# Loading the first 256 columns of w1 in two halves and regrouping the first four units of a dense-SiLU-dense kernel

## The chip, the cores and the metric

The kernel runs on one core of one Trainium2 chip. The core has a matrix engine (TensorE, PE in the profile), a vector engine (DVE), a scalar engine (ACT), GpSimd (POOL) and SyncE (SP), which here only issues transfers. Sixteen DMA engines move data between HBM and the core's SBUF. Transfers are issued from two places, SP and ACT, and each has its own DMA queue (q1 and q10 in the profile); both queues feed the same sixteen engines.

The metric is the device time of one execution in microseconds. Before the change it is 126.83 us, the median of three runs (126.76 to 126.91).

## The reference

A two-layer feed-forward block in bf16, x of 2048 x 640, w1 of 640 x 1728, w2 of 1728 x 640:

```
h = jnp.einsum("bsd,df->bsf", x, w1)
h = _silu(h)
out = jnp.einsum("bsf,fd->bsd", h, w2)
```

## The kernel before

The program writes its order by hand. A small `Plan` (lines 21 to 72) collects operations in program order. Each engine then runs its own operations in that order, and waits on a semaphore only where an operation names another as its dependency. Each transfer, or group of transfers, has a semaphore of its own. Nothing is reordered by a scheduler, so the order in the source is the order of each engine.

The first product is computed transposed: h's columns lie on partitions, x's rows along the free axis. For this x is needed transposed (`xT_sb`, five tiles of 128 of the 640 inner columns by 2048 rows). Rows are worked in four chunks of 512 (`SCH`), w1's 1728 columns in 13 column tiles of 128 and a last one of 64.

A *unit* (line 205) is one column tile against some rows. It takes the next of eight PSUM banks in turn (`take_bank`), and issues five matmuls that accumulate over the 640 inner columns (line 209). Then ACT computes a sigmoid of the bank (line 193), and DVE multiplies the bank by it into `hT_sb` (line 196). The first matmul of a unit carries all the unit's waits: for its rows of xT, for its column tile of w1 (`w1_deps`, line 183) and for its bank.

The head of the program fills the core's memory:

- x's first 512 rows come as four tiles of 128 rows (`load_x0`, line 144), issued in turn from SP, ACT, SP, ACT. TensorE transposes them (line 167), and DVE and ACT copy the results to `xT_sb` (lines 173 and 175). Five and a bit warm-up matmuls on a constant precede them (line 158).
- w1 comes in groups of column tiles (`w1_cuts`, line 136, and `load_w1`, line 148). The first group, column tiles 0 and 1, is issued from ACT, behind its two tiles of x. The other groups, tiles 2 and 3, 4 to 7 and 8 to 13, are issued from SP, which first waits until the third tile of x has landed.
- The other rows of x are transposed on the way by the DMA engines (line 231), issued from SP after a wait for the group of column tiles 4 to 7; w2 is loaded between them (lines 238 and 241).

The first four units work on half chunks: column tiles 0 and 1 against the first 256 rows, then column tiles 0 and 1 against the next 256 (`XE` is 256). They stand in lines 244 to 246. From column tile 2 on, each unit takes a whole chunk of 512 rows (line 248). Then come the chunks 1 to 3, the last column tile for all chunks (line 219), and the second product (line 289) with its evictions and stores.

Of the kernel before, what the change touches and what calls it, by code (L numbers as in the profile page):

```python
# [20 lines left out]
class Plan:  # L21
# [9 lines left out]
    def add(self, eng, emit, deps=(), group=None):  # L31
        op = Op(eng, emit, [d for d in deps if d is not None], group)
        self.ops.append(op)
        return op
# [40 lines left out]
def bass_standalone__dense_activation_silu__prompt_kernel(  # L75
# [19 lines left out]
    FT = FR + 1  # L95
# [7 lines left out]
    with ExitStack() as es:  # L103
# [29 lines left out]


        XE = 2 * P
        w1_cuts = [0, 2, 4, 8, FT]
        id_a = add("pool", lambda e: e.memset(ident[:, :], 0.0))
        id_b = add("pool", lambda e: e.affine_select(
            out=ident[:, :], in_=ident[:, :], compare_op=ALU.not_equal, fill=1.0,
# [4 lines left out]
        def load_x0(eng, j):  # L144
            return add(eng, lambda e: e.dma_start(  # L145
                out=x0_sb[:, j, :], in_=x0_v[:, j, :]), group=f"x0_{j}")

        def load_w1(eng, g, deps=()):
            f0, f1 = w1_cuts[g] * P, min(w1_cuts[g + 1] * P, F)
            return add(eng, lambda e: e.dma_start(  # L150
                out=w1_sb[:, :, f0:f1], in_=w1_v[:, :, f0:f1]), deps, group=f"w1_{g}")

        x0_of = [load_x0(eng, j) for j, eng in enumerate(("sp", "act", "sp", "act"))]
        w1_dma = [load_w1("act", 0)] + [load_w1("sp", g, [x0_of[2]]) for g in (1, 2, 3)]

        ones = nc.const_aps.tensor(1.0, [P, SCH], bf16)
        for n in [SCH] * 5 + [2 * P]:
# [47 lines left out]
        def unit(sc, ft, c0, n):  # L205
            b = take_bank()
            cols = slice(sc * SCH + c0, sc * SCH + c0 + n)
            for dt in range(DT):
                pe = add("pe", lambda e, dt=dt: e.matmul(  # L209
                    ps[:, b, 0:n], lhsT=w1_sb[:, dt, ft * P:(ft + 1) * P], rhs=xT_sb[:, dt, cols],  # L210
                    start=(dt == 0), stop=(dt == DT - 1)),
                    x_deps(sc, c0, n) + w1_deps(ft) + bank_free[b] if dt == 0 else ())
            silu(b, [(slice(0, P), ft, cols)], n, pe)
# [15 lines left out]
        for sc in range(1, NSC):  # L229
            for dt in range(DT):  # L230
                x_dma[sc] = add("sp", lambda e, sc=sc, dt=dt: e.dma_start_transpose(
                    out=xT_sb[:, dt, sc * SCH:(sc + 1) * SCH],
                    in_=xf[sc * SCH:(sc + 1) * SCH, dt * P:(dt + 1) * P]),
                    [w1_dma[2]], group=f"x{sc}")
            if sc == 2:
                half = FR // 2
                for a, z in ((0, half), (half, FR)):
                    w2_dma.append(add("sp", lambda e, a=a, z=z: e.dma_start(
                        out=w2_sb[:, a:z, :], in_=w2_v[:, a:z, :]), group="w2"))
                for hh in range(2):  # L240
                    w2_dma.append(add("sp", lambda e, hh=hh: e.dma_start(
                        out=w2_sb[hh * H:(hh + 1) * H, FR, :], in_=w2[FR * P:F, :]), group="w2"))

        for c0 in (0, XE):
            for ft in range(2):
                unit(0, ft, c0, XE)
        for ft in range(2, FR):
            unit(0, ft, 0, SCH)
# [116 lines left out]
```

## Time and profile before

| What | Value |
|---|---|
| median of three runs | 126.83 us (126.76 to 126.91) |
| time of the profiled execution | 127.35 us |
| its span, first to last instruction | 126.0 us |
| TensorE busy | 121.2 us, 96% of the span |
| DVE, ACT busy | 47.6 and 41.5 us |
| granted TensorE clock | 1.000 |
| DMA moved | 10.41 MB in 18665 packets |
| ACT's DMA queue (q10) | 1232 packets, 0.79 MB |
| issue of the first w1 group on ACT, to landing | 4.3 us |
| issue of w1's tiles 2 and 3 on SP, to landing | 4.9 us |

The profiled execution's time is 1.35 us longer than its span, and 0.52 us above the median of the runs. Positions are given in microseconds from the start of the span. Matmuls are pipelined, so the busy time of one matmul is longer than its distance from the next: in the steady part 512-column matmuls follow each other at about 0.216 us (49 matmuls and the pipeline's end in 10.74 us, with a few records missing). A wait in the profile is the idle time of an engine before an instruction, with what released it. A wait is only worth something where the chain of work that ended last runs through it.

### The profile page before, as it was taken

The page shows a single profiled execution, that of the slowest core. Times are in us where ns is not written, and L with a number is a line of the kernel's source. Part 1 is how long each engine was busy: PE and PEld are TensorE (multiplying, and loading weights), DVE is VectorE, ACT ScalarE, POOL GpSimd, SP SyncE. Part 2 cuts the span into 40 slices and gives each one's busy share as a digit, 9 for nine tenths or more (in the row PEclk, how much of TensorE's full clock was granted, in tenths as well). Part 3 has the DMA queues.
Part 4 walks back from the last instruction along what each step waited for, and adds up shares of the span by engine and source line. Part 5 has one row for each costly group of instructions (what it writes and reads, how often), then busy time and mean ns, then how long its engine had stood idle before and what let it go on. Part 6 is the DMA issues. An engine that isn't in the chain of part 4 may idle for free.

```text
span 126.0 us, 2112 instructions
## 1 busy us (share of the span) xinstructions
PE 121.2 (96%) x905; PEld 57.9 (46%) x910; DVE 47.6 (38%) x74; ACT 41.5 (33%) x73; POOL 0.7 (1%) x6
## 2 busy tenths in 40 slices
PE   7689999999999999999999999999999999999992
PEld 2564444444444444444444444444444444445482
DVE  0454666666666666666674020202020210202022
ACT  4444555555555555555550010101010110101021
POOL 2000000000000000000000000000000000000000
PEclk9999999999999999999999999999999999999999
DMA  4898825379970000000000001113230200112415
GB/s 127 237 271 303 99 53 113 87 182 382 280 136 0 5 0 3 0 0 0 0 0 5 0 0 23 35 21 117 102 109 0 104 0 21 26 21 72 156 65 148
DMA packets 18665, 10.41 MB, mean 83 GB/s; under 512 B 11744, under 2 KB 18656, under 8 KB 18656
## 3 DMA queue, kind: packets, MB, share of 16 engines
q1 hardware_dynamic: 17424, 9.49, 28.5%
q10 hardware_dynamic: 1232, 0.79, 2.1%
q8 instruction: 7, 0.11, 0.4%
q14 instruction: 2, 0.02, 0.0%
HBM read 5.16 MB, written 2.62 MB: 62 GB/s over the span
## 4 chain that ended last, share of the span: by engine, by line
PE 91%; DMA 6%; issue 0%; SPq 0%; DVE 0%
PE ps L289 46%; PE ps L209 43%; DMA w_sb<-in_w_dram 4%; DMA x_sb<-in_x_dram 2%; PE ps L219 2%; SPq L145 0%; DVE o_sb L300 0%
## 5 line engine op out<-in xcount | busy, mean ns | idle before, releaser
L209 PE MATMUL ps<-xT_sb,w_sb 128*128 128x512 bf16 (+1 forms) x265 | 56.2, 371 | 1.6 <-DMA w_sb<-in_w_dram 1.3
L196 DVE TENSOR_TENSOR hT_sb<-ps,sig_sb 128x512 bf16<-128x512 f32 (+2 forms) x58 | 39.0, 673 | 23.2 <-ACT sig_sb L193 22.8
L289 PE MATMUL ps<-w_sb,hT_sb 64*128 64x512 bf16 (+2 forms) x486 | 47.3, 352 | 0.0
L193 ACT ACTIVATE sig_sb<-ps 128x512 bf16<-128x512 f32 (+1 forms) x56 | 32.6, 582 | 27.7 <-PE ps L209 26.6
L209 PEld LDWEIGHTS ps<-xT_sb,w_sb 128*128 128x128 bf16 x270 | 26.3, 98 | 31.2 <-DVE xT_sb L173 1.2
L289 PEld LDWEIGHTS ps<-w_sb,hT_sb 64*128 64x128 bf16 x486 | 23.1, 94 | 23.9
L300 DVE CAST o_sb<-ps 128x512 bf16<-128x512 f32 (+2 forms) x9 | 5.7, 632 | 37.6 <-PE ps L289 37.6
L302 ACT CAST o_sb<-ps 128x512 bf16<-128x512 f32 (+2 forms) x9 | 4.8, 539 | 38.6 <-PE ps L289 38.6
L289 PE MATMUL ps<-hT_sb,w_sb 64*128 64x512 bf16 x108 | 12.3, 376 | 0.0
L289 PEld LDWEIGHTS ps<-hT_sb,w_sb 64*128 64x128 bf16 x108 | 5.1, 94 | 6.6 <-issue 0.4
L300 DVE CAST oT_sb<-ps 128x512 bf16<-128x512 f32 x2 | 1.4, 692 | 11.7 <-PE ps L289 11.7
L302 ACT CAST oT_sb<-ps 128x512 bf16<-128x512 f32 x2 | 1.2, 586 | 13.6 <-PE ps L289 13.6
L158 PE MATMUL ps<-const-bfloat16-1.0 128*128 128x512 bf16 (+1 forms) x6 | 2.5, 588 | 0.8 <-PEq L350 0.8
L173 DVE COPY xT_sb<-ps 128x384 bf16<-128x384 bf16 x4 | 1.4, 358 | 3.2 <-PE ps L167 3.2
L219 PE MATMUL ps<-xT_sb,w_sb 128*64 128x512 bf16 x20 | 2.3, 381 | 0.0
L167 PE MATMUL ps<-ident,x_sb 128*128 128x128 bf16 x20 | 2.0, 267 | 0.1
L175 ACT COPY xT_sb<-ps 128x256 bf16<-128x256 bf16 x4 | 1.4, 372 | 2.0 <-PE ps L167 2.0
L167 PEld LDWEIGHTS ps<-ident,x_sb 128*128 128x128 bf16 x20 | 1.6, 125 | 0.8 <-DMA x_sb<-in_x_dram 0.8
L219 PEld LDWEIGHTS ps<-xT_sb,w_sb 128*64 128x64 bf16 x20 | 1.0, 110 | 1.2 <-issue 0.4
L158 PEld LDWEIGHTS ps<-const-bfloat16-1.0 128*128 128x128 bf16 x6 | 0.7, 133 | 1.9 <-issue 1.9
L142 ACT ACT_TABLE_LOAD x1 | 1.3, 1283 | 0.7 <-PEq L350 0.7
L141 DVE MEMSET warm_sb<- 128x32 f32 x1 | 0.1, 85 | 0.8 <-PEq L350 0.8
(7 smaller groups left out, 1.1 us busy)
## 6 DMA issues: line engine op xcount, KB each, us to landing
out_dram<-o_sb SPq DMA_DIRECT2D x14, 160.0 KB, 1.9
w_sb<-in_w_dram SPq DMA_DIRECT2D x1, 1120.0 KB, 7.7
w_sb<-in_w_dram SPq DMA_DIRECT2D x1, 960.0 KB, 5.7
w_sb<-in_w_dram SPq DMA_DIRECT2D x1, 880.0 KB, 8.0
w_sb<-in_w_dram SPq DMA_DIRECT2D x1, 640.0 KB, 6.3
x_sb<-in_x_dram SPq DMA_DIRECT2D x2, 160.0 KB, 2.5
x_sb<-in_x_dram ACTq DMA_DIRECT2D x2, 160.0 KB, 2.9
w_sb<-in_w_dram ACTq DMA_DIRECT2D x1, 320.0 KB, 4.3
```

Source lines behind the costliest of these rows:

```text
L142: add("act", lambda e: e.activation(out=warm_sb[:, :], in_=warm_sb[:, :], func=ACT.Sigmoid), [warm])
L158: add("pe", lambda e, n=n: e.matmul(ps[:, NBANK - 1, 0:n], lhsT=ones[:, 0:P], rhs=ones[:, 0:n], start=True, stop=True))
L167: t = add("pe", lambda e, j=j, b=b, dt=dt, d0=d0: e.transpose(ps[:, b, :].bitcast(bf16)[:, (dt - d0) * P:(dt - d0 + 1) * P], x0_sb[:, j, d ...
L173: c = add("dve", lambda e, src=src, dst=dst: e.tensor_copy(out=dst, in_=src), [t])
L175: c = add("act", lambda e, src=src, dst=dst: e.copy(out=dst, in_=src), [t])
L193: a = add("act", lambda e: e.activation(out=sig_sb[:, s, 0:n], in_=ps[:, b, 0:n], func=ACT.Sigmoid), [pe, sig_free[s]])
L196: v = add("dve", lambda e, rows=rows, ft=ft, cols=cols: e.tensor_tensor(out=hT_sb[rows, ft, cols], in0=ps[rows, b, 0:n], in1=sig_sb[rows, ...
L209: pe = add("pe", lambda e, dt=dt: e.matmul(ps[:, b, 0:n], lhsT=w1_sb[:, dt, ft * P:(ft + 1) * P], rhs=xT_sb[:, dt, cols], start=(dt == 0), ...
L219: pe = add("pe", lambda e, dt=dt, hh=hh: e.matmul(ps[hh * H:(hh + 1) * H, b, :], lhsT=w1_sb[:, dt, FR * P:F], rhs=xT_sb[:, dt, (sc + hh) * ...
L289: pe = add("pe", lambda e, b=b, n=n, lhsT=lhsT, rhs=rhs, ft=ft: e.matmul(ps[:, b, 0:n], lhsT=lhsT, rhs=rhs, start=(swap == 0 and ft == 0), ...
L300: ev = add("dve", lambda e, b=b, n=n, dst=dst: e.tensor_copy(out=dst, in_=ps[:, b, 0:n]), [pe])
L302: ev = add("act", lambda e, b=b, n=n, dst=dst: e.copy(out=dst, in_=ps[:, b, 0:n]), [pe])
```

## The change

The first group of w1's columns is cut in two: column tile 0 and column tile 1 are two transfers, one behind the other on ACT's queue. The groups on SP keep their columns and only shift in number. The first four units are regrouped: column tile 0 against rows 0 to 255 and 256 to 511, then column tile 1 against both. Through `w1_deps` each column tile waits for its own transfer. The wait of x's transposes is written from the end of the list, and means the same group of column tiles (4 to 7) as before.

```diff
-        w1_cuts = [0, 2, 4, 8, FT]
+        w1_cuts = [0, 1, 2, 4, 8, FT]
...
-        w1_dma = [load_w1("act", 0)] + [load_w1("sp", g, [x0_of[2]]) for g in (1, 2, 3)]
+        w1_dma = [load_w1("act", 0), load_w1("act", 1)] + [load_w1("sp", g, [x0_of[2]]) for g in (2, 3, 4)]
...
-                    [w1_dma[2]], group=f"x{sc}")
+                    [w1_dma[-2]], group=f"x{sc}")
...
-        for c0 in (0, XE):
-            for ft in range(2):
+        for ft in range(2):
+            for c0 in (0, XE):
                 unit(0, ft, c0, XE)
```

## The prediction

> **What bounds the kernel now.** I read the page first, then the chain of waits, then the opening 14 us in slices with the DMA queues beside them. The page's table of engine shares says that TensorE is busy nearly always:
>
> ```profile
> PE 121.2 (96%) x905; PEld 57.9 (46%) x910; DVE 47.6 (38%) x74; ACT 41.5 (33%) x73; POOL 0.7 (1%) x6
> ```
>
> So the only time to win or lose is where TensorE stands still, and the chain that ended last (start, length, what) says where:
>
> ```profile
> 1.19 2.73 DMA x_sb<-in_x_dram
> 3.92 0.02 issue
> 3.94 4.93 DMA w_sb<-in_w_dram
> 8.87 0.05 issue
> 8.92 0.82 PE ps L209 x3
> ...
> 63.05 2.28 PE ps L219 x20
> 65.33 58.47 PE ps L289 x594
> ```
>
> The reader is to see that two transfers make the head of the chain. x0's third tile lands at 3.92; this lets SP issue column tiles 2 and 3 of w1 at 3.94; they land at 8.87. From 8.92 to 123.80 there is nothing but TensorE. Whatever delays the landing at 8.87 delays the end by as much, and whatever happens in front of it is free unless it lasts beyond it. Call that landing the gate.
>
> The order of time in front of the gate, TensorE alone (start, length, work, idle before it and what ended it):
>
> ```profile
> 4.78 0.45 PE L167 MATMUL ps<-ident,x_sb 128*128 128x128 bf16 x5
> 6.25 2.35 PE L209 MATMUL ps<-xT_sb,w_sb 128*128 128x256 bf16 x20 [1.02 <-DMA w_sb<-in_w_dram]
> 8.92 1.25 PE L209 MATMUL ps<-xT_sb,w_sb 128*128 128x512 bf16 x4 [0.32 <-DMA w_sb<-in_w_dram]
> ```
>
> The 20 matmuls at 6.25 are the four units that the change regroups. They waited 1.02 us for the first w1 transfer, ended at 8.60, and then TensorE waited 0.32 us more for the gate. Both waits are on w1, but only the second is on the chain: the first is not.
>
> The DMA engines in the same stretch (window, then the busy sums; the last two columns are the share of 16 engines and GB/s):
>
> ```profile
> 4.00:5.00 1.00, 0.85 (x13) 0.68 (x11) 0.72 (x3) 0.84 (x3) 0.00 (x0) 1.00 0.79 218
> 5.00:6.00 1.00, 0.23 (x5) 0.05 (x1) 0.36 (x1) 0.41 (x2) 0.00 (x0) 1.00 0.72 178
> 6.00:7.00 1.00, 0.75 (x7) 0.71 (x8) 0.00 (x0) 0.00 (x1) 0.00 (x0) 1.00 0.99 268
> ```
>
> They are nearly full, so more DMA work here has little room. Who used them, from the queue table (packets, MB, share of 16 engines) of the window 4 to 5, where ACT's queue is alone:
>
> ```profile
> q10 hardware_dynamic: 427, 0.22, 78.6%
> ```
>
> And, for a price, of the window 18 to 22, where SP's queue carries transposes of x alone:
>
> ```profile
> q1 hardware_dynamic: 1684, 0.40, 46.3%
> ```
>
> **The change part by part.**
>
> *The split of the transfer.* One transfer of [128, 5, 256] columns has 128 x 5 = 640 rows of 512 B; two of 128 columns have 1280 rows of 256 B. The bytes stay, the packets double. The price of a 512 B packet: 78.6% of 16 engine-us over 427 packets = 29.5 ns. A plain 256 B load is not in this trace. Lower bound: the transposes, whose packets average 0.40 MB / 1684 = 238 B, took 46.3% of 64 engine-us over 1684 = 17.6 ns, in another kind of transfer. Upper bound: no cheaper than 512 B, 29.5 ns. I take the middle, 23.6 ns, since one row has the right size and the other the right kind. Extra DMA work: (1280 x 23.6 - 640 x 29.5) ns / 16 = 0.71 us; with the ends 0.23 and 1.18 us.
>
> What can hide it: the engines' idle share while SP's transfer comes up. In quarter slices from 5.00 to 6.25 the share was 0.71, 0.73, 0.73, 0.70 and 0.96, so 1.17 x 0.25 = 0.29 us stood empty. I let all of it be filled, because from 6 to 7 the engines reach 0.99. The rest competes with the gate's own 640 packets, which begin at about 5.1: 0.71 - 0.29 = **0.42 us later at the gate**. Ends: 0.23 - 0.29, taken as 0, and 1.18 with nothing filled.
>
> [...]
>
> *One more DMA issue on ACT.* The issue of the w1 transfer took 0.46 us, from 1.84 to 2.30. A second one ends at about 2.76. Behind it on ACT stands the first copy of xT, which began at 3.86 because the transposes were late. Cover 1.1 us, cost nothing; without the cover 0.46 us, at a place that is in front of the gate anyway.
>
> *SP and POOL.* SP issues the same transfers in the same order; the transposes of x still wait for the transfer of column tiles 4 to 7. POOL is untouched. The transfer for tiles 4 to 7 landed by 10.72, where SP's wait for it ends, and is wanted at 8.92 + 10 x 0.216 = 11.08: 0.36 us of slack that moves with the gate. x's second 512 rows: the fifth transpose was issued at 17.28 and lands some 3.0 us on, at 20.3, against a need at 8.92 + 55 x 0.216 = 20.8. It hangs on the same landing, so it moves along too.
>
> *Column tile 0 first.* The second and third unit change places; the count of matmuls, weight loads, sigmoids, multiplies and banks is the same. The first half's data: ACT's queue had its x rows off at about 3.85 and ran at 78.6%, so by 5.1 it moves 1.25 x 0.786 x 16 / 0.0236 = 666 packets of 256 B. The first half is through at 5.1 and, with the 0.45 us that the whole transfer needed from its last packet (5.75) to its landing (6.2), there at 5.5. The last copies of xT end at 5.64. Column tile 0 runs from about 5.6 to 6.7 (0.54 us a unit, from the sigmoids' starts at 7.00, 7.54, 8.09 and 8.63). This removes most of the 1.02 us wait, and is worth nothing: TensorE only comes earlier to the next wait.
>
> *The added wait for the second half.* In TensorE's queue, column tile 1 and all later matmuls stand behind it; ACT and DVE wait for these. About 610 packets are left at 5.1, 0.90 engine-us. Through the ramp up to 6.0 some 0.52 of that fits; the rest goes at half rate against SP's packets, to 6.8; landing 7.2. Column tile 1 then ends at 8.3, a us before the gate at 8.87 + 0.42 = 9.29. Not on the path.
>
> **Sum.** Removed from the chain 0; added 0.42 us at its head. The profiled execution has a span of 126.0 and a time of 127.35; the median of the runs shown is 126.83, 0.5 below it. Span 126.4, profiled time 127.8, median 126.83 + 0.42 = 127.25.
>
> **The rivals.** What a measurement of this kernel can tell from no change is about 0.2%, 0.25 us.
>
> *Hidden, no change.* The 256 B packets cost what the transposes' do, 0.23 us, and this goes into the 0.29 us of idle share: 126.83. For: a size-true row of the trace. Against: those packets had the queue nearly alone and half-idle engines.
>
> *The second half becomes the gate.* The landing at 8.87 came 1.9 us after the mean engine had moved its 640 packets (10 + 32 + 43 + 88 + 123 by 6.25, 347 more by 7.0), so one engine lags. If the second half, off at 6.8, lags alike, it lands at 8.7, and column tile 1 runs until 8.7 + 1.1 = 9.8 in place of 8.92: +0.9 us, 127.7. It decides once the second half lands after 9.29 - 1.1 = 8.2. Against: the first transfer lagged by 0.45 us only.
>
> *Faster.* The 1.9 us of lag are the one thing at the gate that could shrink. If other packets on ACT's queue change which engine falls behind, and 0.8 us of it goes, the gate comes at 8.87 + 0.42 - 0.8 = 8.5: -0.4 us, 126.4. It counts from a landing before 8.62. For: the share of 1.48 in 8.0 to 8.5 shows packets held up on some engines. Against: nothing on SP's queue changes, and ACT's queue gets no lighter. Without an earlier gate no gain is possible, however early column tile 0 runs.
>
> **How the numbers follow.** Forecast (the gate late by 0.25 to 1.2 us) 0.44; second half as the gate 0.17; hidden 0.26; faster 0.13. Slower 0.44 + 0.17 = 0.61, same 0.26, faster 0.13. The predicted time is the forecast's, 127.25, whose own range is 127.08 to 128.0. The range for all is 126.5 to 128.2: below it lies about half of the faster case (0.07), above it the upper part of the second-half case, where a lag of more than 2.4 us is needed (0.08).
>
> **What would show it.** Right: ACT's queue with 1232 + 640 + 16 = 1888 packets (16 per transfer for its completion; 1232 = 2 x 128 + 640 + 2 x 128 + 5 x 16); column tile 0 starting at 5.5 to 5.8; the second wait of TensorE on w1 in the midst of the small matmuls; the wait before the first 512-column matmul grown from 0.32 us to about 1; the chain still through SP's transfer, landing near 9.3; from there the same 114.9 us of TensorE. Wrong: a landing at 8.9 or before it (hidden, faster), the chain running through ACT's second half (rival), or matmuls of other lengths after the gate, which I have not reckoned with. The weakest number is the 23.6 ns; each ns of it is 0.08 us.

## The result, and the profile after

The change makes the kernel faster by a little: 126.44 us (126.16 to 127.19, 20 runs) against 126.78 us (126.45 to 128.68, 20 runs) for the kernel before. The medians are 0.34 us apart, and the ratio is 0.9975, 95% interval 0.9964 to 0.9986. One run of the kernel before, at 128.68 us (1.8% above its fastest, 126.45), counts as slow and is left out of the ratio. A loss of 0.42 us was forecast, and the range began at 126.5. The direction was wrong, and the time lies just below the range.

The profiled execution of the changed kernel took 126.71 us with a span of 125.4. Its chain that ended last (start, length, what):

```profile
0.73 0.04 issue
0.77 2.50 PE ps L158 x6
3.28 2.30 PE ps L167 x20
5.58 0.13 issue
5.71 56.70 PE ps L209 x270
62.41 2.28 PE ps L219 x20
64.69 58.47 PE ps L289 x594
```

No transfer is on it any more: the chain goes from the warm-up through the transposes into the first unit at 5.71, and from there TensorE works to the end. The first unit's start hangs on a transfer all the same. Column tile 0 landed at 5.57, just before the end that the profile gives the transposes (5.58), and the table below shows which of the two set the start. In the kernel before the same chain ran through x's third tile and the gate. The changed kernel's TensorE and weight loads in the order of time (start, length, work, idle before it):

```profile
5.71 6.63 PE L209 MATMUL ps<-xT_sb,w_sb 128*128 128x256 bf16 x38
```

```profile
7.45 0.64 PEld L209 LDWEIGHTS ps<-xT_sb,w_sb 128*128 128x128 bf16 x6
8.28 1.62 PEld L209 LDWEIGHTS ps<-xT_sb,w_sb 128*128 128x128 bf16 x9 [0.19 <-DMA w_sb<-in_w_dram]
```

The wait of 1.02 us before the first small matmul is gone, and so is the wait of 0.32 us before the first 512-column one. The gate (the landing of column tiles 2 and 3, as the prediction calls it) still shows in the weight loads, which stood 0.19 us for it; it was issued at 4.04 and took 4.2 us to land, so it was there at 8.24, 0.6 us before the 8.87 of the trace before.

ACT's queue in the window 4 to 5 (packets, MB, share of 16 engines), and over the whole span:

```profile
q10 hardware_dynamic: 884, 0.23, 104.6%
```

```profile
q10 hardware_dynamic: 1888, 0.79, 2.3%
```

In the same microsecond 884 packets moved as many bytes as 427 did before (0.23 and 0.22 MB). The packets are the 1888 that were reckoned. One of them took 1.046 x 16 us / 884 = 18.9 ns on average.

So there were two things to find out. Why is an earlier start of column tile 0 worth something, if the gate stands behind it? And did the split bring the gate forward, or did it land at 8.87 in the one trace by chance of that execution?

### The profile page after: what moved, and what is told of

It reads as the page before. It is cut to its first block, busy times and chain, and to the rows that moved or that the text cites. A ratio compares the mean times of both kernels' runs of the same rounds, so it can differ in the third digit from the quotient of the medians.

```text
span 125.4 us, 2118 instructions
## 1 busy us (share of the span) xinstructions
PE 122.2 (97%) x910; PEld 58.7 (47%) x910; DVE 47.6 (38%) x74; ACT 41.6 (33%) x73; POOL 0.7 (1%) x6
## 3 DMA queue, kind: packets, MB, share of 16 engines
q10 hardware_dynamic: 1888, 0.79, 2.3%
## 4 chain that ended last, share of the span: by engine, by line
PE 98%; DVE 0%; issue 0%
PE ps L289 47%; PE ps L209 45%; PE ps L158 2%; PE ps L167 2%; PE ps L219 2%; DVE o_sb L300 0%
```

## The experiments

Theory A: the gain is TensorE's earlier start, and the gate's landing differs from execution to execution. Theory B: the split itself brings the gate forward. Each kernel was timed beside the kernel before on the same chip, and traced once. The first four went together; the kernel before took 126.81 us there.

**The kernel before, traced again.** No edit.

> The kernel before once more, unaltered, for a second trace of it. Theory A (TensorE's earlier start on column tile 0 is the gain; where the gate, the transfer of column tiles 2 and 3, lands is a matter of the execution): time 126.8 us, the gate lands somewhere between 8.2 and 8.9, so the 0.32 us wait before the first 512-column matmul may be gone here, and then the first w1 wait of about 1 us is on the chain. Theory B (the split itself brings the gate forward, 8.9 to 8.3): 126.8 us, the gate lands at 8.9 again, within 0.2.

Measured: 126.6 us, ratio 0.9987 [0.9962, 1.0013], span 125.0. Its chain:

```profile
1.83 3.80 DMA w_sb<-in_w_dram
5.63 0.14 issue
5.76 2.99 PE ps L209 x23
8.76 0.05 issue
8.81 3.40 PE ps L209 x15
```

This is the same program, and another transfer is on the chain. The first w1 transfer landed at 5.63 (6.12 in the first trace), the gate, issued at 4.40, 3.3 us later at 7.74 (8.87). TensorE never waited for the gate. What ended the wait on the chain was the transfer that the prediction had put off the path. Theory B expected 8.9 again and has no support here; Theory A had the waits right, but its 8.2 to 8.9 for the gate was too late as well.

**The split alone, with and without the earlier start.** The first edit has two transfers, the old order of units, and a first unit that waits for both; the second has two transfers and the old order, each unit waiting for its own column tile. Against the changed kernel:

```diff
-        return [w1_dma[max(g for g in range(len(w1_dma)) if w1_cuts[g] <= ft)]]
+        return [w1_dma[max(g for g in range(len(w1_dma)) if w1_cuts[g] <= max(ft, 1))]]
...
-        for ft in range(2):
-            for c0 in (0, XE):
+        for c0 in (0, XE):
+            for ft in range(2):
                 unit(0, ft, c0, XE)
```

> Two transfers of 128 columns as in the changed kernel, but the old order of units, and the first unit waits for both. Theory A: TensorE starts its small matmuls at 6.1 to 6.3 as before, so nothing is won: 126.8 us. Theory B: the gate lands near 8.3, the small matmuls end at 8.6, so the 0.3 us wait at the gate is gone: 126.5 us. My theory on record (256-byte packets dear, 23.6 ns): 127.2 us.

```diff
-        for ft in range(2):
-            for c0 in (0, XE):
+        for c0 in (0, XE):
+            for ft in range(2):
                 unit(0, ft, c0, XE)
```

> Two transfers of 128 columns, the old order of units (column tile 0, then 1 on the first 256 rows, then both on the next). Theory A: the first unit starts at 5.7 like in the changed kernel; the second needs column tile 1, which lands at about 6.2, when the first unit ends; so all or nearly all of the gain: 126.4 to 126.5 us. Theory B: the same, 126.4 to 126.5. If the order of the units carries the gain: 126.7 to 126.8.

Measured: 126.89 us, 1.0004 [0.9981, 1.0027], with the wait for both; 126.55 us, 0.9978 [0.9956, 1.0], without it. These two move the same packets by the same transfers and differ in one wait alone, and the difference of the medians, 0.34 us, is that of the whole change. With twelve runs each the two intervals overlap, so these times alone do not settle it; the traces have to show where the difference arises. Chains, first of the kernel that waits for both:

```profile
2.26 0.07 issue
2.33 3.36 DMA w_sb<-in_w_dram
5.69 0.14 issue
5.83 2.99 PE ps L209 x23
```

and of the one that does not:

```profile
3.28 2.15 PE ps L167 x20
5.43 0.12 issue
5.55 2.34 PE ps L209 x20
7.89 0.01 issue
7.90 0.82 PE ps L209 x3
```

With the wait for both, the second transfer is on the chain: it landed at 5.69, and the first unit started at 5.83. Without it the chain names the transposes, but column tile 0 landed at 5.41 and the first unit started at 5.55, by the same 0.14 us behind the landing that it needs. So the start moved by 0.28 us with the landing. The gate landed at about 7.9 in both (7.93 and 7.86), so the split does not carry the gain by the gate. In the second trace the four units were done sooner than that, and the gate held the next matmul by 0.17 us, so the two spans differ by 0.1 us only (125.1 and 125.0). The price on record (127.2 us) has no support either: 1280 packets in place of 640, with nothing won in return, gave 126.89 against 126.81.

**The order alone.** One transfer as before, units in the new order.

```diff
-        for c0 in (0, XE):
-            for ft in range(2):
+        for ft in range(2):
+            for c0 in (0, XE):
                 unit(0, ft, c0, XE)
```

> One transfer of 256 columns as before, the new order of units. Both theories: nothing, 126.8 us, small matmuls from about 6.2 on, since both column tiles land together. If the order carries the gain: 126.4.

Measured: 126.81 us, 1.0001 [0.9977, 1.0025]. The order is worth nothing by itself, and with the old order the split has its gain (126.55), so it is not shown to be worth anything beside the split.

The next four went together, with 127.0 us for the kernel before.

**The gate made late.** In the changed kernel:

```diff
-        w1_dma = [load_w1("act", 0), load_w1("act", 1)] + [load_w1("sp", g, [x0_of[2]]) for g in (2, 3, 4)]
+        w1_dma = [load_w1("act", 0), load_w1("act", 1)] + [load_w1("sp", g, [x0_of[3]]) for g in (2, 3, 4)]
```

> The changed kernel with its gate made late: SP issues column tiles 2 and 3 only after x's fourth tile has landed (near 4.8) in place of the third (near 4.0). Theory A (the gain is TensorE's earlier start; the gate, which lands between 7.9 and 8.9 by the execution, stands just beside the path): the gate lands at 8.7 to 9.3, TensorE waits 0.4 to 1 us for it, and the gain is gone: 126.8 to 127.2 us. Rival C (the gate has room to spare and the front is bound by TensorE alone): 126.4 to 126.5 us.

Measured: 126.41 us, 0.996 [0.9941, 0.9979], span 124.7. This was a miss of the experiment's own aim: the gate did not come late. It was issued later, at 4.43, and landed earlier, 3.1 us on at 7.49, and nothing waited for it. So its time, which is in Rival C's range, does not decide between the two. The chain (the first matmul of the first unit started at 5.43, beside the end that the profile gives the transposes):

```profile
3.28 2.18 PE ps L167 x20
5.46 3.00 PE ps L209 x23
```

and the gate's line in the table of issues (KB, us from issue to landing):

```profile
w_sb<-in_w_dram SPq DMA_DIRECT2D x1, 320.0 KB, 3.1
```

**The price of 256-byte rows on the gate.** Two kernels load the gate in two transfers, both waited for; one cuts the columns (256-byte rows), the other the inner dimension (512-byte rows).

```diff
-        w1_cuts = [0, 2, 4, 8, FT]
+        w1_cuts = [0, 2, 3, 4, 8, FT]
...
-        w1_dma = [load_w1("act", 0)] + [load_w1("sp", g, [x0_of[2]]) for g in (1, 2, 3)]
+        w1_dma = [load_w1("act", 0)] + [load_w1("sp", g, [x0_of[2]]) for g in (1, 2, 3, 4)]
...
-        return [w1_dma[max(g for g in range(len(w1_dma)) if w1_cuts[g] <= ft)]]
+        return [w1_dma[max(g for g in range(len(w1_dma)) if w1_cuts[g] <= (3 if ft == 2 else ft))]]
...
-                    [w1_dma[2]], group=f"x{sc}")
+                    [w1_dma[-2]], group=f"x{sc}")
```

> The kernel before with the gate, column tiles 2 and 3, as two transfers of 128 columns (256-byte rows), both waited for before tile 2. Measures the price of the rows where it cannot hide. By the price on record (23.6 ns a packet of 256 B against 29.5 ns of 512 B) the gate's packets need (1280 x 23.6 - 640 x 29.5) / 16 = 0.7 us more than those of the kernel with 512-byte rows beside it: gate 0.5 to 0.7 us later, 127.2 to 127.4 us. If the engines go by bytes: no difference from that kernel, 126.8 to 127.0 us.

```diff
+            if g == 1:
+                add(eng, lambda e: e.dma_start(
+                    out=w1_sb[:, 0:3, f0:f1], in_=w1_v[:, 0:3, f0:f1]), deps, group=f"w1_{g}")
+                return add(eng, lambda e: e.dma_start(
+                    out=w1_sb[:, 3:5, f0:f1], in_=w1_v[:, 3:5, f0:f1]), deps, group=f"w1_{g}")
```

> The control for it: the gate also as two transfers, but cut along the inner dimension (three and two tiles of 128), so the rows keep 512 B. One more issue on SP of about 0.4 us. Both prices: 126.8 to 127.0 us, the gate at most 0.2 us later than in one transfer.

Measured: 127.11 us, 1.0009 [0.9977, 1.0042], by columns, and 127.09 us, 1.0036 [1.0002, 1.007], by the inner dimension; no difference that can be told. The price on record asked for 0.5 to 0.7 us, but the pair did not test it in the time: TensorE did not wait for the gate in either kernel. What both show is the next transfer behind the gate, column tiles 4 to 7, on the chain. By columns:

```profile
4.88 5.95 DMA w_sb<-in_w_dram
10.83 0.05 issue
```

By the inner dimension:

```profile
5.14 5.63 DMA w_sb<-in_w_dram
10.77 0.05 issue
```

From issue to landing it took 0.32 us longer behind the 256-byte rows, but it was issued 0.26 us earlier there. The issue that was added stands in front of it on both chains, with 0.53 us by columns and 0.49 us by the inner dimension. The gate itself landed at 7.88 with 256-byte rows, 4.00 us after its first issue at 3.88, and at 7.50 with 512-byte rows, 3.32 us after 4.18. That is 0.67 us more, about what the price on record gives; but other gates with 512-byte rows took 3.8 to 4.9 us when they were issued at 3.86 to 4.12 (table below), so rows and time of issue are not told apart here.

**The gate on ACT's queue.** The changed kernel, column tiles 2 and 3 third on ACT and without SP's wait:

```diff
-        w1_dma = [load_w1("act", 0), load_w1("act", 1)] + [load_w1("sp", g, [x0_of[2]]) for g in (2, 3, 4)]
+        w1_dma = [load_w1("act", 0), load_w1("act", 1), load_w1("act", 2)] + [load_w1("sp", g, [x0_of[2]]) for g in (3, 4)]
```

> The changed kernel with column tiles 2 and 3 also issued from ACT, third on its queue and without SP's wait for x. Theory A: the gate's data follow at once, it lands near 7.3 to 7.8, always before TensorE has done the first four units at 7.9 to 8.3; what is left is executions of the changed kernel that waited for it: 126.3 to 126.4 us, with less spread. Rival C: 126.4 to 126.5. If ACT's extra issue (0.45 us, ending near 3.4) holds up its copies of xT or x's second tile comes later: 126.7 or more.

Measured: 126.88 us, 0.9975 [0.9942, 1.0009]; a miss. The gate cannot be what was lost, since nothing waited for it. The start was: column tile 0 landed at 6.06 and TensorE stood 1.22 us before the first unit.

```profile
1.83 4.22 DMA w_sb<-in_w_dram
6.06 0.14 issue
6.19 2.99 PE ps L209 x23
```

Why column tile 0 landed later in this one trace was not settled.

The last four went together, with 126.79 us for the kernel before. By then the traces suggested a second thing: Theory D, that the gate lands sooner when it is issued a little later.

> The kernel before, a third trace, on the same chip as the next three. Theory A, now as a sum: let S be the start of the first unit; the span is S + 119.3 us, plus what TensorE then waits for the gate, plus up to 0.3 us where the first unit still runs at half pace. In the traces so far S is 5.8 to 6.3 where both column tiles must have landed and 5.4 to 5.7 where column tile 0 is enough. Expected here: S 5.7 to 6.3, span 125.0 to 126.0, time 126.6 to 127.0 us.

> The changed kernel again. Theory A: S 5.4 to 5.7, set by the end of the transposes and no longer by w1; span 124.7 to 125.2 unless the gate lands after 8.2 or the first unit is at half pace; 0.3 to 0.4 us faster than the kernel before: 126.4 to 126.6 us.

> Changed kernel, SP's loads of w1 held until x's fourth tile has landed, again. Theory D (held a little, the gate comes out of the way of the first w1 transfers and of x, and all of them land sooner: the gate landed at 7.5 when issued at 4.43, at 8.2 to 8.9 when issued at 3.9): 0.15 us or more below the changed kernel beside it, 126.2 to 126.4. Theory A alone (its good time was the execution's luck): within 0.1 us of the changed kernel, or above it where the gate is late.

The fourth is the kernel before with the same hold:

```diff
-        w1_dma = [load_w1("act", 0)] + [load_w1("sp", g, [x0_of[2]]) for g in (1, 2, 3)]
+        w1_dma = [load_w1("act", 0)] + [load_w1("sp", g, [x0_of[3]]) for g in (1, 2, 3)]
```

> The kernel before with the same hold on SP's loads alone. Theory D: the one transfer of both column tiles lands sooner, 5.6 in place of 5.6 to 6.2, and the gate at 7.5 to 7.8: 126.5 us, 0.2 below the kernel before. Theory A alone: the same as the kernel before, 126.7 to 127.0, since S still waits for 256 columns.

Measured, in the same order: 126.94 us, 1.0016 [0.9993, 1.0039]; 126.64 us, 0.9991 [0.9969, 1.0014]; 126.38 us, 0.9964 [0.9945, 0.9983]; 126.75 us, 0.9984 [0.996, 1.0008]. Here the changed kernel is 0.15 us below the shared runs of the kernel before and 0.30 us below its copy. Its interval includes no change and its time stands just above what was expected, so this group by itself does not show the gain. The start was at 5.61, as expected, but not set by the end of the transposes: the profile names the load of w1 (start, length, work, idle before it), and it was column tile 0 that landed just before, at 5.47:

```profile
5.61 6.60 PE L209 MATMUL ps<-xT_sb,w_sb 128*128 128x256 bf16 x38 [0.19 <-DMA w_sb<-in_w_dram]
```

In the same trace the gate is on the chain behind it: it landed at 7.99, and the first 512-column matmul started at 8.04.

The traces in one table, but for those of the three kernels that load the gate in another way. S is the start of the first unit, and the first column the landing of the last w1 transfer that it needs: of column tiles 0 and 1 in the first six rows, of column tile 0 alone in the other five. Landings and starts are taken from the single records of the traces. "Held" is the time from the last small matmul's start to the first 512-column one's, less the 0.11 us that this takes where nothing is waited for. "Pace" is what the twenty small matmuls took, first start to last, beyond the 2.07 us that they take in eight of the eleven traces.

| Kernel | landing for S | S | gate issued, landed | held | pace | span | span - S |
|---|---|---|---|---|---|---|---|
| before | 6.12 | 6.25 | 3.94, 8.87 | 0.48 | 0 | 126.0 | 119.77 |
| before, second trace | 5.63 | 5.76 | 4.40, 7.74 | 0 | 0 | 125.0 | 119.28 |
| before, third trace | 5.66 | 5.80 | 4.04, 7.90 | 0 | 0 | 125.1 | 119.27 |
| order alone | 5.88 | 6.02 | 3.86, 8.26 | 0.11 | 0 | 125.4 | 119.43 |
| split, waits for both | 5.69 | 5.83 | 4.12, 7.93 | 0 | 0 | 125.1 | 119.26 |
| before, loads held | 5.94 | 6.07 | 4.73, 7.87 | 0 | 0.47 | 125.9 | 119.79 |
| split, old order | 5.41 | 5.55 | 3.94, 7.86 | 0.17 | 0 | 125.0 | 119.46 |
| changed | 5.57 | 5.71 | 4.04, 8.24 | 0.08 | 0.32 | 125.4 | 119.67 |
| changed, second trace | 5.47 | 5.61 | 3.91, 7.99 | 0.25 | 0 | 125.2 | 119.60 |
| changed, loads held | 5.29 | 5.43 | 4.43, 7.49 | 0 | 0.04 | 124.7 | 119.30 |
| changed, loads held, second trace | 5.32 | 5.46 | 4.57, 7.71 | 0.12 | 0 | 124.9 | 119.41 |

The sum of Theory A holds: span - S, less what the gate held and what the pace cost, is 119.3 us in every row, within 0.06 us.

S follows the landing by 0.135 or 0.136 us in every row, and in the three kernels left out too (6.06 and 6.19 with the gate on ACT's queue). The end of the transposes shows no such distance: as the profile gives it, it lies in the last five rows from 0.41 us before S (changed, loads held, second trace) to 0.04 us behind it (changed, loads held). So the landing of w1 sets the start with the change as well as without it, and what the change does is to make it the landing of 128 columns in place of 256. Where the chain names the transposes or a copy of xT in place of the transfer, these end close to S by the profile: in the third trace of before and in the held one the copy ended 0.05 and 0.13 us before S, and by the order of the copies it is the last of four, for which the first unit does not wait.

The means of S are 5.96 for the first six rows and 5.55 for the others, 0.41 us apart, and the means of the span 125.4 and 125.0. The gate and the pace take about as much in both groups (0.10 and 0.08 us on average in the first, 0.12 and 0.07 in the second), though in a single trace each can be as large as the gain.

## Why the prediction was wrong

**The reading of the chain.** The step that failed is the first: "Whatever delays the landing at 8.87 delays the end by as much, and whatever happens in front of it is free unless it lasts beyond it." It was right for that execution. But the two waits stood close: the gate held the first 512-column matmul by 0.48 us (the profile's 0.32 us counts from a modelled end of the matmul before), so a gate landing 0.5 us sooner leaves the first w1 wait alone on the chain. It landed 0.6 us sooner or more in all ten other traces of the table. The first trace was the outlier, at 127.35 us itself 0.5 us above the median of the runs, which the prediction noted and did not take as a warning.

**"This removes most of the 1.02 us wait, and is worth nothing."** The start of column tile 0 was reckoned well (5.6; measured 5.71 and 5.61), and so was the landing of its transfer at 5.5 (5.57 and 5.47), in part by luck: with the measured 18.9 ns a packet in place of 23.6 the same reckoning gives an estimate of 5.3. The term was put at nothing and is worth what it removes in a usual execution, some 0.3 to 0.4 us: S comes 0.41 us earlier on average, and the pair with the same transfers and one wait more or less has 0.34 us between its medians.

**The price of a 256-byte packet.** Taken as 23.6 ns, between 17.6 and 29.5; measured 18.9 ns in the changed kernel, against 29.5 and (second trace of before, 583 packets at 101.2%) 27.8 ns for 512 bytes. With 28.6 ns as the mean of these two, the term (1280 x 18.9 - 640 x 28.6) / 16 is 0.37 us and not 0.71, and the idle share of 0.29 us takes nearly all of it. The lower bound, the transposes' packets of nearly the same size, was the nearer one. The 0.42 us at the gate did not show: it was to land at 9.29, and landed at 8.24 and 7.99. For the same bytes the smaller packets took 2 x 18.9 / 28.6 = 1.32 times as long as those of 512 bytes, but no loss of time by it was measured (126.89 us against 126.81 where the first unit waits for both halves).

**Column tile 1.** Expected at 7.2, "a us before the gate". It landed at 6.16 in the changed kernel, which needs it for its third unit at 7.12 only, and no wait for it shows. The rival in which this half becomes the gate fell.

**The faster rival** had the right sign and the wrong place. It asked for a gate landing before 8.62, and said that without an earlier gate no gain is possible. The gate did land earlier in all other traces, with or without the change, and so the early start is what counts.

**Right** were the count of packets (1888 against 1232, 640 more rows and 16 for the transfer that was added), SP's unchanged work, the second issue on ACT (0.55 us from 2.33, in front of nothing) and the work behind the front: the last column tile and the second product take 2.28 and 58.47 us in both kernels.

## What to carry to other kernels

A chain of waits is that of one execution. Where two waits stand within a few tenths of a microsecond on one engine (here the gate held the matmul behind it by 0.48 us), add up the time for either one being early before calling the other free, and ask for a second trace. A profiled execution that took longer than the median of the runs is a warning that its longest transfer may not be the usual one (here 127.35 us against 126.83, with the gate landing at 8.87 against 7.49 to 8.26 in the ten other traces). And a chain that names an engine's own work need not mean that no transfer is behind it: here the distance from a landing to the start of the work, 0.135 or 0.136 us in every trace, told more than the chain of any one.

## What the runs showed of the hardware

In these traces the gate mostly landed earlier when it was issued later. Issued at 3.86 to 4.12, the gate landed between 7.86 and 8.87, 3.8 to 4.9 us on; issued at 4.40 to 4.73, between 7.49 and 7.87, 3.1 to 3.3 us on, with the same bytes in front of it and behind it. Holding SP's loads until x's fourth tile is there made the changed kernel 0.26 us faster beside it (126.38 against 126.64; the ranges of twelve runs, 126.12 to 126.8 and 126.53 to 127.92, overlap), and it was the fastest kernel in both groups that it ran in (126.41 and 126.38). The kernel before gained nothing that can be told from it (126.75 against 126.79), where 0.2 us was expected. In the changed kernel column tile 0 landed at 5.29 and 5.32 with the hold, against 5.57 and 5.47 without; in the kernel before its first w1 transfer landed at 5.94 with the hold, where Theory D expected 5.6, against 5.63 to 6.12 without. So Theory D is borne out by the time of one kernel and not by the other. What happens among the transfers was not settled. In the changed kernel the engines' share in the window 5 to 6 was 0.37 and 0.43 where the loads were held, against 0.85 and 0.92, and the throughput from 7 to 8 and from 8 to 9 was 364 to 378 GB/s against 305 to 350. The changed kernel's first trace (window, busy sums, and last the DMA share and GB/s):

```profile
5.00:6.00 1.00, 0.87 (x8) 0.57 (x6) 0.58 (x2) 0.74 (x2) 0.00 (x0) 1.00 0.85 169
7.00:8.00 1.00, 1.00 (x12) 0.89 (x10) 0.69 (x2) 0.67 (x3) 0.00 (x0) 1.00 1.00 338
```

The same with the loads held (first of its two traces):

```profile
5.00:6.00 1.00, 1.00 (x10) 0.64 (x8) 0.47 (x2) 0.71 (x2) 0.00 (x0) 1.00 0.37 62
7.00:8.00 1.00, 1.00 (x10) 0.78 (x8) 0.73 (x3) 0.68 (x3) 0.00 (x0) 1.00 1.09 372
```

The pace of the first unit also differs by execution. From its start to its first sigmoid it took 0.75 us in most traces (5.76 to 6.51 in the second trace of before), 1.06 us in the changed kernel (5.71 to 6.77) and 1.22 us in the held kernel before (6.07 to 7.29), though the granted clock reads 1.00 throughout. The small matmuls by form, second trace of before and held kernel before:

```profile
L209 PE MATMUL ps<-xT_sb,w_sb 128*128 128x256 bf16 x20 | 2.3, 272 | 0.6 <-DMA w_sb<-in_w_dram 0.6
```

```profile
L209 PE MATMUL ps<-xT_sb,w_sb 128*128 128x256 bf16 x20 | 2.8, 304 | 0.3 <-DVE xT_sb L173 0.3
```

The whole difference lies in the first unit: the sigmoids behind it follow every 0.54 or 0.55 us in all three. It is at most 0.5 us, of the size of the whole change. Within that unit the matmuls of 256 columns start up to 0.21 us apart at first (until 6.46 in the changed kernel, in the held kernel before until 7.09), and 0.11 us apart from then on. The transposes show the same factor of two: they start 0.107 us apart throughout in the changed kernel, and 0.056 us apart from 4.2 on in the first trace of before. So the step came at 4.2, 6.5 and 7.1 us in these three traces. No run here tested its cause.
